# Delta-rule attention and a feed-forward block on one core: loads under a schedule of depths, another model of instruction fetches, and a new order

## The chip, the cores and the metric

The kernel runs on one core of a Trainium2 chip. The metric is the device time of one execution in microseconds (us). Everything below is in us unless marked otherwise.

## The reference

```python
def _attn_ref(q, k, v, beta):            # B, H, S, D = 4, 8, 768, 48
    k_n = k / (np.linalg.norm(k, axis=-1, keepdims=True) + 1e-06)
    state = np.zeros((B, H, D, D), dtype=np.float32)
    for t in range(S):
        kt, vt, bt = (k_n[:, :, t], v[:, :, t], beta[:, :, t, None])
        y[:, :, t] = np.einsum('bhd,bhde->bhe', q[:, :, t], state)
        v_old = np.einsum('bhde,bhd->bhe', state, kt)
        state = state + bt[:, :, :, None] * np.einsum('bhd,bhe->bhde', kt, vt - v_old)
    return y

def _moe_ref(x, w_in, w_out):            # 3072 tokens, 384 -> 2048 -> 384
    h = x @ w_in
    g = h - np.tanh(h)
    return g @ w_out
```

`reference` turns the attention's answer into 3072 rows of 384 numbers and puts them through `_moe_ref`. All inputs and the output are fp32.

## The kernel before

**The work and its pieces.** The 768 steps are cut into 24 chunks of 32 steps, four chunks to a group. A chunk covers 128 tokens (32 steps of 4 batches), a group 512 tokens, which is one window of the feed-forward part. Window 0 is worked in two halves of 256 tokens, the others whole. The 2048 hidden channels are 16 tiles of 128.

**Loads.** All big inputs go through SP's queue (`loads`, L358): keys and queries for the scores (`kc`, `kd`; L315, L322), values (L330), keys in natural order `kt` (L333) and the weights as 32 pieces of 384 KB (`raw`; L354 for `w_in`, L352 for `w_out`). The line `plan.after = plan.flight[-depth[0]][1]` makes a load wait until the load so many places ahead of it has landed; the number is 5 throughout. The planner books each load's time with `transfer` (L263).

**Decoding the weights.** A weight arrives as 8-byte numbers. A piece goes through a Prelu on ScalarE (L814), a byte step on ScalarE (L821) or a shift on VectorE (L824), a word step on VectorE (L826), a cast to the high part (L836, on ScalarE or VectorE) and a subtraction for the low part (L840). Tables by piece (`LOW`, `BYTE`, `CAST`) say which engine.

**The attention.** For each chunk TensorE forms the scores' products k.k and q.k (L406); ScalarE copies them out (L425, L463) or VectorE masks them straight away (L411); the copies are masked by L428. Per group, `solve` (L469) norms the keys (square root on ScalarE, L536), builds a triangular system and solves it on VectorE in pairs of L576 and L578. For group 0 it works in two halves: transposes L589, L594, L598; then for each of its pairs of chunks a join (matmuls L623 and L635, and on VectorE L638, which writes the inverse's off-diagonal block into `tt`). Later groups end in one transpose, L604. The chain then runs chunk by chunk: `keyed` (L681, state times keys), `vsub` (L689), `chunk` (L705), its result copied into `ub` by ScalarE (L721) and VectorE (L723), `update` of the state (L739), copies of the state (L768), the answer (L758) and its copy (L776), and the turn (L792), which is cut into a high part on ScalarE (L799, xh) and a low part on VectorE (L801, xl) for the feed-forward part.

**The feed-forward part.** A hidden block (L869) is nine matmuls of 512 columns (256 in window 0); its gate is tanh on ScalarE (L880), the difference on VectorE (L882), a cast (L888, on either engine) and the rest (L891, VectorE or GpSimd). An out block (L914) is nine more, and the results leave through L945 and L950. Where TensorE has nothing to do, fillers run: L291 (512 columns) and L293 (256), and small pads, L301.

**What sets the order.** The whole program is straight-line code, written out by a planner (`Plan`, L68). Each piece of work is a generator that yields operations with an engine, a cost and what they depend on. The planner emits at each step the operation that can begin first, as adjusted by ranks (`RANKS`, with `TWEAK`, `DUES` and `HOLD` on top). Each engine runs its instructions in the order in which they were emitted. `fetch` (L139) lets a matmul group start later when its instructions reach into a new block of 256, which is taken to arrive after the loads booked so far, but at most 2.2 after the crossing, plus 2.7. `room` and `deep` (L160) say when a load may go out. Tables by tile (`GC`, `GL`, `PREP`) send casts, low parts and the preparing of values to one engine or another.

## Time and profile before

| | us |
|---|---|
| three runs, without a profile | 607.52, 610.75, 609.8 |
| their median | 609.8 |
| the profiled execution | 608.45 |
| its span, first to last instruction | 606.7 |
| around the span | 1.75 |
| TensorE busy in the span | 569.1 (94%) |
| VectorE busy | 364.2 (60%) |
| ScalarE busy | 251.2 (41%) |

The profile comes from one execution, slightly shorter than the median. A row of a timeline gives the start, the length, engine, line, operation, and in brackets the idle time ahead of it with what ended it; "issue" there means nothing that the profile shows. TensorE's and VectorE's busy shares are averages over very different stages: about 61 us of attention alone, some 67 in which the first window's blocks run beside the decoding of the weights, and then the long run of whole windows.

### The profile page before, as it was taken

To read this page: it belongs to the slowest core of one execution; us is meant where nothing else is said; L and a number is where in the kernel's file an instruction comes from. 1 tells how busy PE (TensorE), PEld (TensorE's weight loads), DVE (VectorE), ACT (ScalarE), POOL (GpSimd) and SP (SyncE) were. 2 spreads that over 40 slices of the span, in tenths; PEclk is the share of its full clock that TensorE was granted. 3 is DMA by queue.
4 is the path that set the end of the run, shared out by engine and by line. 5 is a ranking of instruction groups with operands and counts; after the bars stand their busy time and mean duration, and the time that the engine had idled before them with its cause. 6 is when DMAs were issued, how large, how long until landed. Compare 5 with 4: busy or idle time off the path is not lost.

```text
span 606.7 us, 21467 instructions
## 1 busy us (share of the span) xinstructions
PE 569.1 (94%) x9747; PEld 471.5 (78%) x9747; DVE 364.2 (60%) x817; ACT 251.2 (41%) x434; POOL 39.5 (7%) x49
## 2 busy tenths in 40 slices
PE   3567898999999999999999999999999999999997
PEld 3455898989988888777878787787888777887885
DVE  3958799962299932699524998229994232324333
ACT  1546773435443345524354423454324344323332
POOL 1000331001120000010010100001000100000000
PEclk9999899999999999999999999999999999999999
DMA  8986831023321034401234102422001200001001
GB/s 269 300 293 203 283 94 47 14 76 104 111 71 52 1 90 139 124 5 53 75 103 147 32 1 82 134 73 59 1 0 53 73 15 2 1 0 53 1 1 52
DMA packets 25979, 49.88 MB, mean 82 GB/s; under 512 B 3280, under 2 KB 15952, under 8 KB 25888
## 3 DMA queue, kind: packets, MB, share of 16 engines
q1 hardware_dynamic: 25488, 47.95, 25.0%
q8 instruction: 76, 1.25, 0.9%
q10 hardware_dynamic: 400, 0.56, 0.3%
q14 instruction: 15, 0.12, 0.1%
HBM read 43.78 MB, written 4.72 MB: 80 GB/s over the span
## 4 chain that ended last, share of the span: by engine, by line
PE 67%; DVE 21%; DMA 5%; issue 4%; ACT 2%; SPq 0%; ACTq 0%; DVEq 0%
PE ph L869 26%; PE po L914 26%; PE psa L406 4%; DVE ta L576 3%; DVE a L578 3%; PE psu L705 2%; PE psy L758 2%; DVE t L882 2%; PE psk L681 2%; PE sums L739 2%; DVE gh L891 2%; DMA kd<-in_kp 2%; DMA raw<-in_w_in 2%; PE psy L681 2%; DVE a L480 1%
## 5 line engine op out<-in xcount | busy, mean ns | idle before, releaser
L914 PE MATMUL po<-gh,w 128*128 128x512 f32 (+1 forms) x1008 | 218.8, 364 | 1.8 <-ACT o L945 1.0
L869 PE MATMUL ph<-xt,w 128*128 128x512 f32 (+1 forms) x1008 | 216.9, 364 | 2.7 <-DVE t L882 2.0
L869 PEld LDWEIGHTS ph<-xt,w 128*128 128x128 f32 x1008 | 170.0, 190 | 33.6 <-DVE t L882 3.0
L914 PEld LDWEIGHTS po<-gh,w 128*128 128x128 f32 x1008 | 170.0, 190 | 32.4 <-ACT o L945 1.9
L882 DVE TENSOR_TENSOR t<-ph,t 128x512 f32<-128x512 f32 (+1 forms) x112 | 68.5, 612 | 107.0 <-ACT t L880 106.9
L880 ACT ACTIVATE t<-ph 128x512 f32<-128x512 f32 (+1 forms) x112 | 60.2, 537 | 131.6 <-PE ph L869 106.4
L888 ACT CAST gh<-t 128x512 fp32r<-128x512 f32 (+1 forms) x102 | 58.6, 575 | 102.6 <-PE po L914 54.4
L891 DVE TENSOR_TENSOR gh<-t,gh 128x512 fp32r<-128x512 f32 (+1 forms) x107 | 67.6, 633 | 48.8 <-ACT gh L888 48.0
L578 DVE TENSOR_TENSOR a<-a,ta 128x58 f32<-128x58 f32 (+9 forms) x164 | 55.2, 336 | 4.0
L576 DVE TENSOR_TENSOR ta<-a 128x58 f32<-128x58 f32 (+9 forms) x164 | 54.9, 335 | 4.0
L768 ACT COPY st<-sums 48x768 f32<-48x768 f32 x44 | 35.0, 796 | 21.0 <-PE sums L739 19.2
L406 PE MATMUL psa<-kc 48*32 48x64 f32 (+1 forms) x1536 | 28.2, 229 | 11.8 <-issue 8.1
L651 POOL TENSOR_TENSOR v<-v,nt 128x384 f32<-128x384 f32 x21 | 17.8, 854 | 305.3 <-DMA v<-in_vn 299.2
L406 PEld LDWEIGHTS psa<-kc 48*32 48x32 f32 x1536 | 24.2, 119 | 17.2 <-issue 10.4
L721 ACT ACTIVATE ub<-psu,cs 128x384 f32<-128x384 f32 x46 | 24.4, 578 | 24.1 <-PE psu L705 24.1
L705 PE MATMUL psu<-v,tt 32*32 32x48 f32 x1536 | 22.4, 209 | 3.6 <-DVE v L689 3.1
L463 ACT COPY gs<-psa 128x256 f32<-128x256 f32 x20 | 12.3, 614 | 32.6 <-PE psa L406 32.6
L705 PEld LDWEIGHTS psu<-v,tt 32*32 32x32 f32 x1536 | 19.1, 109 | 8.4 <-DVE v L689 4.0
L801 DVE TENSOR_TENSOR xt<-psa,xt 128x384 fp32r<-128x384 f32 x24 | 13.3, 553 | 19.6 <-ACT xt L799 19.6
L739 PE MATMUL sums<-ub,kt 64*48 64x96 f32 x736 | 21.8, 253 | 2.0 <-issue 1.2
L758 PE MATMUL psy<-ub,pc 32*32 32x48 f32 x1536 | 22.6, 208 | 0.4 <-DVE ub L723 0.4
L739 PEld LDWEIGHTS sums<-ub,kt 64*48 64x48 f32 x736 | 16.5, 123 | 8.3 <-issue 6.1
(85 smaller groups left out, 380.8 us busy)
## 6 DMA issues: line engine op xcount, KB each, us to landing
kd<-in_kq SPq DMA_DIRECT2D x23, 448.0 KB, 3.9
kc<-in_kp SPq DMA_DIRECT2D x20, 448.0 KB, 4.8
raw<-in_w_in SPq DMA_DIRECT2D x16, 384.0 KB, 5.3
raw<-in_w_out SPq DMA_DIRECT2D x16, 384.0 KB, 5.8
v<-in_vn SPq DMA_DIRECT2D x24, 192.0 KB, 3.9
kt<-in_kn SPq DMA_DIRECT2D x24, 192.0 KB, 2.7
out<-o SPq DMA_DIRECT2D x17, 256.0 KB, 2.1
kc<-in_kp SPq DMA_DIRECT2D x3, 224.0 KB, 4.9
```

What stands on the lines that cost most here:

```text
L406: nc.tensor.matmul(ps[q, h, :], kc[rows, 0, u, :], kc[rows, x, u, :], start=True, stop=True)
L576: nc.vector.tensor_tensor(tv, P(slice(j + 1, size), slice(j, j + 1)).broadcast_to(dims), top.broadcast_to(dims), ALU.mult)
L578: nc.vector.tensor_tensor(rest_, rest_, tv, ALU.add)
L705: nc.tensor.matmul(pu[rows, h, :], tt[rows, 8 * r + h, :], v[rows, h, :], start=True, stop=True)
L739: nc.tensor.matmul(to, kt[rows, h, :], ub[rows, h], start=(s == 0 and h < 2), stop=True, skip_group_check=True)
L768: (nc.vector.tensor_copy if eng == "DVE" else nc.scalar.copy)(st[rows, :, :, hp, :], ps)
L869: nc.tensor.matmul(p, wi[f][:, a, ct, :], xt[:, b, ct, part], start=(ct == 0 and i == 0), stop=(ct == NC - 1 and i == 2))
L880: nc.scalar.activation(t_, p, AF.Tanh)
L882: nc.vector.tensor_tensor(t_, p, t_, ALU.subtract)
L888: (nc.vector.tensor_copy if on_dve else nc.scalar.copy)(gh[:, 0, :n], t_)
L891: hw_.tensor_tensor(gh[:, 1, :n], t_, gh[:, 0, :n].bitcast(F32), ALU.subtract)
L914: nc.tensor.matmul(po[c][:, part], wo[f][:, a, 128 * c:128 * c + 128], gh[:, b, :n], start=(f == 0 and i == 0 and z < 1), stop=(f == NF - ...
```

## The change

The planner's model of three things changes, and all its tables are replaced.

- `fetch`: a block of instructions now arrives 2.45 after the later of the crossing plus 0.6 and the end of the loads booked so far less 0.4. The bound of 2.2 is gone.
- `room`: the number of loads under way follows the planner's time. It is 5 until 9.9, 2 until 22.25, 3 until 43.47, and 5 after that. In the program as built, the loads from raw 1's first half to raw 1's second half wait for the load two places ahead, those from raw 2's first half to raw 7's second half for three, and the others for five.
- `transfer`: 330 GB/s in place of 290, and 0.85 to land in place of 0.4.
- Constants, ranks, dues and the tables by tile have new numbers. 25 casts of the gate are on VectorE where it was 10, 12 of the rest on GpSimd where it was 5, 5 low parts of weights on GpSimd where it was 4, and 4 values are prepared on VectorE where it was 3. The fillers of 512 columns are 38 where they were 17, those of 256 columns 7 where they were 24, and the pads 16 where they were 34.

All real work is the same. From L160 on a line of the kernel before has a number that is higher by one than in the changed kernel.

```diff
@@ fetch
-            lines.append(max(at + 1.4, min(self.dma[0], at + 2.2)) + 2.7)
+            lines.append(max(at + 0.6, self.dma[0] - 0.4) + 2.45)
@@ room, deep
-        n = self.deep()
-        return self.flight[-n][0] if len(self.flight) >= n else 0.0
-
-    def deep(self):
-        return QUIET if self.calm() else FLIGHT
+        for n, a, b in zip(DEPTHS, (0.0,) + PHASES, PHASES + (1e9,)):
+            t = max(a, self.free["SP"], self.flight[-n][0] if len(self.flight) >= n else 0.0)
+            if t < b:
+                return t, n
@@ transfer
-        plan.dma[0] = max(plan.dma[0], end + 1.5) + kb * 1024e-3 / 290.0
-        return Event(plan.dma[0] + 0.4)
+        plan.dma[0] = max(plan.dma[0], end + 1.5) + kb * 1024e-3 / 330.0
+        return Event(plan.dma[0] + 0.85)
@@ loads
-                    depth[0] = plan.deep()
-                    return plan.room()
+                    t, depth[0] = plan.room()
+                    return t
@@ tables
-FLIGHT, QUIET, FILL0, SOON, HASTE, PADT, RIDE = 5, 5, 1.89, 28.48, 0.4, 13.27, 0.38
+DEPTHS, PHASES = (5, 2, 3, 5), (9.9, 22.25, 43.47)
+FILL0, SOON, HASTE, PADT, RIDE = 1.99, 29.03, 0.13, 19.04, 0.32
-GC = [int(x) for x in "10000110011010000000101000000011"]
+GC = [int(x) for x in "11111011011111110110110110111101"]
-    "score": (-20.93, -84.55, -7.16), "gram": (-38.65, -104.48, -99.64), "solve": (-76.22, -172.04, -61.98),
+    "score": (-46.64, -87.64, -2.97), "gram": (-36.29, -173.12, -95.32), "solve": (-89.51, -149.32, -32.24),
...
```

Three places show how the order moves. The first is the start of solve(0). On ScalarE, from its seventh instruction on, before (`psa` is a product in PSUM, `pc` its copy, `nm` the norm, `raw0` weight piece 0):

```order
L536 ACTIVATE nm_289<-ss_290 128x32
L425 COPY pc_336<-psa_252 128x256
L814 ACTIVATE raw0_247<-raw0_247 128x768
L547 ACT_TABLE_LOAD
L547 ACTIVATE wz_79<-wz_79 128x1
L821 ACTIVATE raw0_247<-raw0_247,cs_76 128x768
```

And now:

```order
L424 COPY pc_328<-psa_250 128x256
L535 ACTIVATE nm_286<-ss_287 128x32
L424 COPY pc_368<-psa_295 128x256
L813 ACTIVATE raw0_247<-raw0_247 128x768
L820 ACTIVATE raw0_247<-raw0_247,cs_76 128x768
```

Two copies of products are ahead of piece 0's Prelu where it was one, and one of them is ahead of the square root. On VectorE, from the building of the triangle (L561) on, before (`a0` is the triangle, `ta` its scratch):

```order
L561 SCALAR_TENSOR_TENSOR a0_287<-a0_287,gm_293 128x16x16 x2
L576 TENSOR_TENSOR ta_78<-a0_287 128x28
L578 TENSOR_TENSOR a0_287<-a0_287,ta_78 128x2x14
L576 TENSOR_TENSOR ta_78<-a0_287 128x52
L578 TENSOR_TENSOR a0_287<-a0_287,ta_78 128x2x13x2
L576 TENSOR_TENSOR ta_78<-a0_287 128x72
```

And now, with piece 0's word, cast and low part (`w0`) in between:

```order
L560 SCALAR_TENSOR_TENSOR a0_284<-a0_284,gm_290 128x16x16 x2
L825 SCALAR_TENSOR_TENSOR raw0_247<-raw0_247 128x768
L575 TENSOR_TENSOR ta_78<-a0_284 128x28
L577 TENSOR_TENSOR a0_284<-a0_284,ta_78 128x2x14
L835 CAST w0_406<-raw0_247 128x2x384
L575 TENSOR_TENSOR ta_78<-a0_284 128x52
L577 TENSOR_TENSOR a0_284<-a0_284,ta_78 128x2x13x2
L839 TENSOR_TENSOR w0_406<-raw0_247,w0_406 128x2x384
L575 TENSOR_TENSOR ta_78<-a0_284 128x72
```

Two masks (L410) and piece 1's word follow further down in the same solve, all ahead of its first transpose. The second place is VectorE behind the solve, from the first transpose to the first join of `tt`, before (`v` are values, `pc` scores, `raw` and `w` weights):

```order
L589 STREAM_TRANSPOSE tt0_506<-a0_287 128x16x32
L594 STREAM_TRANSPOSE ta_78<-a0_287 128x16x32
L598 STREAM_TRANSPOSE tt0_506<-a0_287 128x16x32
L651 TENSOR_TENSOR v_100<-v_100,nt_294 128x384
L651 TENSOR_TENSOR v_137<-v_137,nt_294 128x384
L428 TENSOR_TENSOR pc_432<-pc_432,cs_76 128x256
L428 TENSOR_TENSOR pc_460<-pc_460,cs_76 128x256
L824 TENSOR_SCALAR raw3_438<-raw3_438 128x768
L826 SCALAR_TENSOR_TENSOR raw0_247<-raw0_247 128x768
L428 TENSOR_TENSOR pc_336<-pc_336,cs_76 128x256
L638 SCALAR_TENSOR_TENSOR tt0_506<-psa_593,cs_76,tt0_506 128x8x16
```

And now:

```order
L588 STREAM_TRANSPOSE tt0_579<-a0_284 128x16x32
L593 STREAM_TRANSPOSE ta_78<-a0_284 128x16x32
L597 STREAM_TRANSPOSE tt0_579<-a0_284 128x16x32
L650 TENSOR_TENSOR v_99<-v_99,nt_291 128x384
L427 TENSOR_TENSOR pc_404<-pc_404,cs_76 128x256
L427 TENSOR_TENSOR pc_368<-pc_368,cs_76 128x256
L427 TENSOR_TENSOR pc_328<-pc_328,cs_76 128x256
L650 TENSOR_TENSOR v_103<-v_103,nt_291 128x384
L839 TENSOR_TENSOR w1_585<-raw1_292,w1_585 128x2x384
L823 TENSOR_SCALAR raw3_581<-raw3_581 128x768
L825 SCALAR_TENSOR_TENSOR raw2_478<-raw2_478 128x768
L637 SCALAR_TENSOR_TENSOR tt0_579<-psa_671,cs_76,tt0_579 128x8x16
```

A third mask, a low part and a word of piece 2 stand ahead of the first join where piece 0's word stood, and piece 3's shift is still among them. The third place is TensorE around the first chunks, before from update 0 on (`psa` from `tt0` and `yj` are the joins, `psk` and `psy` with `st` the keyed products):

```order
L739 MATMUL sums_80<-ub_677,kt_102 48x2x48 x16
L623 MATMUL psa_705<-tt0_506,gs0_89 32x16 x32
L758 MATMUL psy_744<-ub_677,pc_432 32x48 x32
L792 MATMUL psa_783<-cs_76,y_sb_779 128x128 x3
L635 MATMUL psa_790<-yj_777,ta_78 32x16 x32
L291 LDWEIGHTS wz_79
L291 MATMUL po0_82<-wz_79 128x512
L681 MATMUL psk_842<-st_77,kd1_175 32x96 x16
L681 MATMUL psy_843<-st_77,kd1_175 32x96 x16
L705 MATMUL psu_891<-v_137,tt0_506 32x48 x32
```

And now, from the first join's matmuls to chunk 0:

```order
L622 MATMUL psa_592<-tt0_579,gs0_89 32x16 x32
L622 MATMUL psa_629<-tt0_579,gs0_89 32x16 x32
L634 MATMUL psa_671<-yj_667,ta_78 32x16 x32
L634 MATMUL psa_713<-yj_709,ta_78 32x16 x32
L290 LDWEIGHTS wz_79
L290 MATMUL po0_82<-wz_79 128x512
L704 MATMUL psu_748<-v_99,tt0_579 32x48 x32
```

Both joins now stand ahead of chunk 0; the second one's matmuls stood between update 0 and keyed 1.

## Rows read from the trace of the kernel before

**Rows 1.** Table of stretches: start and end, length, then the busy time of TensorE, its weight loads, VectorE, ScalarE and GpSimd (with instructions), the granted TensorE clock, the DMA engines' busy share, and GB/s.

```profile
0.00:61.28 61.28, 37.22 (x1337) 28.15 (x1337) 41.07 (x89) 27.82 (x41) 3.18 (x10) 1.00 0.82 264
64.07:127.69 63.62, 60.16 (x1193) 56.76 (x1194) 58.79 (x150) 32.01 (x63) 11.55 (x9) 0.97 0.30 98
127.69:600.00 472.31, 466.35 (x7189) 382.49 (x7189) 260.71 (x576) 187.61 (x324) 22.80 (x29) 1.00 0.18 56
```

**Rows 2.** TensorE's waits from 0 to 110: what waited, for what, total us, times, longest.

```profile
PE psa L406 <- issue: 10.3, 4, 3.9
```

**Rows 3.** The page's DMA queues: packets, MB, share of 16 engines.

```profile
q8 instruction: 76, 1.25, 0.9%
```

**Rows 4.** TensorE's timeline, the scores' products and the first join: start, length, line, idle ahead in brackets.

```profile
19.42 1.60 PE L406 MATMUL psa<-kc 48*32 48x32 f32 x99 [3.87 <-issue]
...
32.36 0.58 PE L406 MATMUL psa<-kc 48*32 48x64 f32 x10 [3.69 <-issue]
32.87 1.10 PE L623 MATMUL psa<-tt,gs 32*32 32x16 f32 x64
```

**Rows 5.** VectorE's timeline, solve(0) and its first join.

```profile
16.71 0.20 DVE L576 TENSOR_TENSOR ta<-a 128x28 f32<-128x28 f32 x1
...
25.28 1.06 DVE L589 STREAM_TRANSPOSE tt<-a 128x512 f32<-128x512 f32 x1
...
36.84 0.35 DVE L638 SCALAR_TENSOR_TENSOR tt<-psa,cs,tt 128x128 f32<-128x128 f32 x1 [5.51 <-PE psa L635]
```

**Rows 6.** TensorE's timeline from chunk 0 to the first hidden block.

```profile
37.25 1.50 PE L705 MATMUL psu<-v,tt 32*32 32x48 f32 x64 [0.48 <-DVE tt L638]
...
40.11 1.53 PE L739 MATMUL sums<-ub,kt 64*48 64x96 f32 x32 [0.81 <-DVE ub L723]
...
49.47 1.51 PE L681 MATMUL psk<-st,kd 112*32 112x96 f32 x32
...
59.45 1.10 PE L406 MATMUL psa<-kc 48*32 48x64 f32 x64
...
61.28 2.42 PE L869 MATMUL ph<-xt,w 128*128 128x256 f32 x18
```

**Rows 7.** VectorE's instructions from 28 to 62, grouped by line: busy us, mean ns of one, idle ahead.

```profile
L826 DVE SCALAR_TENSOR_TENSOR raw<-raw 128x768 int32<-128x768 int32 x9 | 8.6, 956 | 0.0
L840 DVE TENSOR_TENSOR w<-raw,w 128x768 fp32r<-128x768 f32 x7 | 6.7, 954 | 0.1
L824 DVE TENSOR_SCALAR raw<-raw 128x768 int32<-128x768 int32 x4 | 2.3, 564 | 0.0
L836 DVE CAST w<-raw 128x768 fp32r<-128x768 f32 x4 | 2.2, 552 | 0.0
...
L428 DVE TENSOR_TENSOR pc<-pc,cs 128x256 f32<-128x256 f32 x3 | 1.2, 435 | 0.0
L801 DVE TENSOR_TENSOR xt<-psa,xt 128x384 fp32r<-128x384 f32 x2 | 1.1, 558 | 1.1 <-ACT xt L799 1.1
...
L651 DVE TENSOR_TENSOR v<-v,nt 128x384 f32<-128x384 f32 x2 | 1.0, 544 | 0.0
```

**Rows 8.** ScalarE's timeline around solve(0), and the state's copy after update 0.

```profile
13.79 0.23 ACT L536 ACTIVATE nm<-ss 128x32 f32<-128x32 f32 x1 [10.02 <-DVE ss L511]
15.19 0.37 ACT L425 COPY pc<-psa 128x256 f32<-128x256 f32 x1 [1.17 <-PE psa L406]
15.77 0.89 ACT L814 ACTIVATE raw<-raw 128x768 f32<-128x768 f32 x1 [0.21 <-DMA raw<-in_w_in]
...
18.09 0.96 ACT L821 ACTIVATE raw<-raw,cs 128x768 int32<-128x768 uint8 x1
...
43.20 0.79 ACT L768 COPY st<-sums 48x768 f32<-48x768 f32 x1 [1.33 <-DVE st L768]
```

**Rows 9.** All 16 loads of `w_in`, time from issue to landing.

```profile
DMA to landing us min/median/max: 3.5/5.3/7.1
```

**Rows 10.** VectorE's instructions from 64 to 128, grouped by line: busy us, mean ns of one, idle ahead.

```profile
L882 DVE TENSOR_TENSOR t<-ph,t 128x256 f32<-128x256 f32 x21 | 8.7, 417 | 0.5 <-ACT t L880 0.5
...
L888 DVE CAST gh<-t 128x256 fp32r<-128x256 f32 x6 | 1.7, 289 | 0.0
```

**Rows 11.** TensorE's timeline near the end of window 0's overlap, and chunk 4.

```profile
122.85 1.24 PE L914 MATMUL po<-gh,w 128*128 128x256 f32 x9
123.93 2.32 PE L869 MATMUL ph<-xt,w 128*128 128x256 f32 x18
...
131.02 0.88 PE L705 MATMUL psu<-v,tt 32*32 32x48 f32 x64
```

**Rows 12.** TensorE's timeline at the end of window 0: the last turn and what follows it.

```profile
172.60 0.55 PE L792 MATMUL psa<-cs,y_sb 128*128 128x128 f32 x3
172.91 4.79 PE L869 MATMUL ph<-xt,w 128*128 128x256 f32 x27
```

**Rows 13.** TensorE's weight loads, timeline, at the last out block.

```profile
600.82 1.68 PEld L914 LDWEIGHTS po<-gh,w 128*128 128x128 f32 x8 [0.33 <-DVE gh L891]
```

**Rows 14.** SP's timeline, three issues: start, length in the queue, what is loaded.

```profile
27.56 5.74 SPq L315 DMA_DIRECT2D kc<-in_kp  x2
...
54.56 0.33 SPq L330 DMA_DIRECT2D v<-in_vn  x1
61.41 0.33 SPq L333 DMA_DIRECT2D kt<-in_kn  x1
```

More of the change, by code (lines that the diff above doesn't have):

```diff
@@ L1009 @@
+GL = [int(x) for x in "11010101101000000000101000110010"]
 BYTE = [int(x) for x in "1110111001010111"]
-PREP = [int(x) for x in "0010"]
-CAST = [int(x) for x in "1011001010010000"]
-GC = [int(x) for x in "10000110011010000000101000000011"]
+PREP = [int(x) for x in "0000"]
+CAST = [int(x) for x in "1010011010100000"]
+GC = [int(x) for x in "11111011011111110110110110111101"]
 RANKS = {
-    "mask": (-32.37, -37.91, 7.1), "answers": (-14.24, -55.53, -1.28), "moved": (29.15, -23.48, -15.77),
-    "score": (-20.93, -84.55, -7.16), "gram": (-38.65, -104.48, -99.64), "solve": (-76.22, -172.04, -61.98),
-    "join": (-0.8, 19.48, 32.82), "prep": (-62.42, 24.49, 50.59), "keyed": (-78.17, -12.19, -47.04),
-    "chunk": (-3.89, 32.79, 20.73), "update": (21.42, -29.13, -22.09), "answer": (55.51, 34.26, 60.41),
-    "vsub": (-41.91, -5.88, 54.2), "spread": (-38.17, -40, 8.2), "keep": (8.64, 39.88, 21.97),
-    "y": (23.84, 0.77, 57.29), "turn": (-10.04, -17.53, 8.95), "xh": (-11.76, 23.09, 117.67),
-    "xl": (12.12, -26.31, 22.22), "raw": (-49.09, -24.09, -28.31), "word": (-7.84, -79.58, -20.8),
-    "high": (9.94, -11.13, -38.28), "low": (11.13, -23.86, 42.85), "hidden": (21.81, -34.31, -15.76),
-    "out": (-34.25, -11.58, -0.19), "tanh": (-21.22, 10.97, 42.16), "lw": (-32.26, -8.41, -32.05),
[3 rows of a table removed]
@@ L1026 @@
-HOLD = [11.87, 1.73, 0]
+    "mask": (-51.4, -25.44, -4.49), "answers": (-11.29, -23.17, -37.84), "moved": (82.62, -19.37, -94.63),
+    "score": (-46.64, -87.64, -2.97), "gram": (-36.29, -173.12, -95.32), "solve": (-89.51, -149.32, -32.24),
+    "join": (14.87, -22.33, 84.36), "prep": (-50.27, -23.5, 58.14), "keyed": (-110.02, -19.62, -21.59),
+    "chunk": (-39.43, 13.76, 9.17), "update": (9.24, -7.15, -20.24), "answer": (15.23, 56.56, 16.95),
+    "vsub": (25.27, -6.27, 39.52), "spread": (-32, -48.21, -32.63), "keep": (-35.35, -16.32, 63.96),
@@ L1027 @@
+    "y": (16.21, 29.92, 104.72), "turn": (-12.05, -15.64, 30.52), "xh": (-50.88, 7.05, 53.86),
+    "xl": (5.76, -71.85, 42.14), "raw": (-39.7, 4.39, -0.22), "word": (7.02, -7.26, 33.55),
+    "high": (7.19, -7.02, -1.45), "low": (26.91, -44.7, 47.28), "hidden": (37.9, -28.65, -41.88),
+    "out": (-12.65, -18.77, -7.35), "tanh": (-54.48, -15.76, 34.42), "lw": (-18.65, -49.35, -9.34),
[3 rows of a table added]
+HOLD = [9.94, 36.8, 0]
 DUES = {
-    "x0": 9.364, "x1": 31.018, "x2": 63.17, "x3": 85.053, "x4": 121.817, "r4": 5.942, "p4": 87.319, "u0": 56.841,
@@ L1036 @@
-    ("chunk", 2): -11.69, ("chunk", 3): -39.11, ("chunk", 4): 19.01, ("chunk", 5): 6.92, ("chunk", 6): -6.29,
+    ("answers", 9): -0.02, ("answers", 10): 0.14, ("answers", 11): 4.34, ("chunk", 0): -46.83, ("chunk", 1): 22.61,
+    ("chunk", 2): -26.82, ("chunk", 3): -32.39, ("chunk", 4): 19.01, ("chunk", 5): 6.92, ("chunk", 6): -6.29,
     ("chunk", 7): 1.2, ("chunk", 8): -1.87, ("chunk", 9): 4.69, ("chunk", 10): -5.27, ("chunk", 11): -0.1,
-    ("gate", -1): 5.11, ("gate", 0): 30.18, ("gate", 1): -9.36, ("gh", -1): -2.8, ("gh", 0): -22.27,
@@ new lines @@
+    ("moved", 11): -0.74, ("out", -1): 3.94, ("out", 0): -17.63, ("out", 1): 4.98, ("prep", 0): 16.17,
+    ("prep", 1): -44.38, ("prep", 2): 2.09, ("prep", 3): -77.75, ("prep", 4): -0.23, ("prep", 5): -5.22,
+    ("prep", 6): -0.07, ("prep", 7): 3.65, ("prep", 8): -3.06, ("prep", 9): 0.51, ("prep", 10): -2.75,
+    ("prep", 11): -0.01, ("raw", 0): -9.18, ("raw", 1): -3.4, ("raw", 2): -27.43, ("raw", 3): -6.13,
+    ("raw", 4): -45.36, ("raw", 5): -7.67, ("raw", 6): 43.75, ("raw", 7): -8.14, ("raw", 8): 20.28,
@@ new lines @@
+    ("raw", 9): -28.37, ("raw", 10): -28.85, ("raw", 11): -13.28, ("raw", 12): -82.62, ("raw", 13): 6.46,
+    ("raw", 14): -25.43, ("raw", 15): 10.45, ("score", 0): 0.11, ("score", 1): 2.47, ("score", 2): -1.45,
+    ("score", 3): 1.9, ("score", 4): 17.38, ("score", 5): 19.28, ("score", 6): -10.65, ("score", 7): 47.27,
+    ("score", 8): -0.02, ("score", 9): -5.02, ("score", 10): 1.82, ("score", 11): -2.03, ("solve", 0): -6.69,
+    ("solve", 4): 50.53, ("solve", 8): -55.42, ("solve", 12): -76.11, ("solve", 16): -28.82, ("solve", 20): -48.75,
```

134 lines of the change are left out of this document (62 added, 72 removed), and 74 rows, old and new, of tables (RANKS, TWEAK).

## The prediction

> **What bounds the kernel now.** I read the table of stretches first [rows 1]. From 127.69 to 600.00 TensorE is busy 466.35 of 472.31 us: nothing but its own work counts there, and the change neither adds to nor takes from that work. The loss lies ahead. Up to the first hidden block at 61.28 TensorE is busy 37.22 us, fillers included, and from 64.07 to 127.69 VectorE is busy 58.79 of 63.62 us. So the sum is about two things: when the first hidden block starts, and how long VectorE's queue is between there and chunk 4.
>
> Next I read what TensorE waited for early on [rows 2]. The largest entry, 10.3 us, is "issue" ahead of the products: the engine waited for nothing that has a semaphore. In TensorE's own sequence [rows 4] such a wait stands inside a group of equal matmuls (99 of the scores' products after 3.87 us at 19.42, 10 more after 3.69 us at 32.36), where the next instruction, not its data, is missing. I take these as waits for the next block of instructions: a queue of its own brings them, 76 packets of together 1.25 MB or 16 KB each [rows 3], and meanwhile the loads keep the DMA engines busy (share 0.82 up to 61.28 [rows 1]). The change's depths and its new fetch line bear on this.
>
> Third comes the chain to the first hidden block: solve(0) on VectorE from 16.71, its first transpose ending at 25.28 + 1.06 = 26.34 [rows 5], joins from 32.87 [rows 4], chunk 0 at 37.25, update 0 at 40.11, keyed 1 at 49.47, hidden at 61.28 [rows 6].
>
> **Step 1, up to the first transpose of solve(0).** Before, that transpose ends at 26.34 and the joins still wait until 32.87 for the block; only the block counts. The change moves weight decoding into VectorE's part of the solve: two words at 0.956, one cast at 0.552, one low part at 0.954 [rows 7], and two masked products, taken like L428 at 0.435: 1.91 + 0.55 + 0.95 + 0.87 = +4.3. On ScalarE the copy of one score (15.19, 0.37) now precedes the square root, which stood at 13.79 [rows 8]: the root goes to 15.56, +1.8. And the first word needs raw 0's Prelu (0.89) and byte (0.96) [rows 8], which now stand behind a second copy, of a product behind the block that came at 19.42. That block's wait shows no price for its new place. Between all but 0.5 of its 3.87 us removed and none, it comes at 16.0 to 19.4; I take 17.5, the middle, since five loads are still in flight there. With 0.7 for its product (44 of the 99 matmuls that took 1.60), 0.37, 0.89 and 0.96 the word starts at 20.4, where VectorE would otherwise be ready at 16.71 + 1.8 = 18.5: 1.9 idle (0.4 to 3.8). The transpose ends at 26.34 + 4.3 + 1.8 + 1.9 = **34.3** (32.8 to 36.2). Two loads in flight then should bring the block of 32.36 well before that; TensorE's extra 512-column fillers lie in that wait. It would count again only if it came after 34.3. So the block wait is replaced by VectorE, and the joins start 1.4 later than 32.87. GpSimd gains low parts of later windows, hidden.
>
> **Step 2, to chunk 0.** Before the first join of tt on VectorE (L638, 36.84) there now stand two more transposes (1.06 each), two values (0.544 each), three masks (0.435), a low part, a shift (0.564) and a word: 2.1 + 1.1 + 1.3 + 0.95 + 0.56 + 0.96 = 7.0 [rows 5, 7], and the join's 0.35: chunk 0 at 34.3 + 7.3 = **41.6** (40 to 43.5), 4.4 after before's 37.25. Both joins' matmuls run beneath it. Depth 2 holds SP, and behind it stand raw 1's second half, the keys of chunks 6 and 7 and raw 2, whose word is due at about 40. Raw 0 lands by 15.77 [rows 8]; nine loads of 393 or 459 KB at 264 GB/s [rows 1] take some 15, and raw 2 is there by 32. If two in flight starve the engines (5.3 from issue to landing [rows 9], so 2.65 a load), it comes at 40 and chunk 0 slips by up to 2; that is the upper bound.
>
> **Step 3, chunk 0 to the first hidden block.** Before: 61.28 - 37.25 = 24.0. There keyed 1 at 49.47 stood behind joins, answer and turn, while the state was ready at 43.20 + 0.79 = 43.99 [rows 6, 8]: 5.5. After, both joins are already done and three fillers (some 0.6) stand there: -4.9. The product at 59.45 (1.0 from its start to the next) moves behind the hidden block: -1.0. So 18.1, and hidden starts at 41.6 + 18.1 = **59.7**, -1.6 (55.5 to 62.5).
>
> **Step 4, hidden block to chunk 4.** VectorE has more ahead of solve(1)'s end than before: six more L882 at 0.417 and fourteen more casts L888 at 0.289 [rows 10], two words, a low part, two shifts and a cast [rows 7], less one L891: 2.5 + 4.05 + 1.9 + 0.95 + 1.1 + 0.55 - 0.5 = 10.6. By this queue chunk 4 comes at 131.02 - 1.6 + 10.6 = 140.0. But TensorE has also done 12 more hidden and out half blocks by then; one takes 123.93 - 122.85 = 1.08 [rows 11], 13.0 in all. At equal progress chunk 4 would come at 144.0, so VectorE's sum says -4.0. If TensorE kept all of its idle time there, only step 3's -1.6 would stay. VectorE is busy 92% of this stretch, so I take -3.5, near its end (-6 to +1, with step 3's bounds).
>
> **Steps 5 and 6.** At the end of window 0, three half blocks of window 0 (172.91, x27) stand between the last turn (172.60) and the next window [rows 12]; in the changed order none do. The hidden block then waits for two casts, about 0.56 each by L801 [rows 7], and their hand-overs: +1.3. At the end, the last out block waits for its gate until 600.82, with five fillers ahead [rows 13]; in the changed order three other out blocks stand before it: -0.95. 330 GB/s and 0.85 of landing are planner's numbers and cost nothing by themselves; the gates moved from ScalarE to VectorE after 131 lie under TensorE.
>
> **The sum.** -3.5 + 1.3 - 0.95 = -3.15 on the profiled execution's 608.45 (606.7 of span and 1.75 around it): 605.3. The median of the three runs is 1.35 higher, so 606.65.
>
> **Rivals.**
> A, faster: short fetches and small groups at their later pace. The 64 small matmuls of a chunk took 1.50 at 37.25 and 0.88 at 131.02 [rows 6, 11], although the clock column reads 1.00 in the row that covers the first and in that of the second [rows 1]; I can't say from these rows why. If fillers (17 of 512 columns become 38) bring the small groups to the later pace, eight groups between chunk 0 and hidden (chunks, updates, keyed, answers) give 8 x 0.6 = 4.9, and no idle in step 1 gives 1.5 more. Hidden at 53 to 54; with about 5 of it kept, 601.5. Against it: the fillers stand ahead of the joins and thin out behind them.
>
> B, slower: the loads end too late. SP issues in order, and the changed order has 13 weight loads behind kt of chunk 3 where it was 8; that kt waits for update 1, just ahead of the hidden block (61.41, where the load before it went at 54.56 [rows 14]). Five loads of 393 KB at 264 GB/s [rows 1] are 7.4 us. ScalarE has the Prelus of these weights in order between its tanhs, so the gates stall with them. It decides from the point where a weight lands after ScalarE reaches its Prelu; then 606.65 + 7.4 = 614. For it: at depth 3 an issue-to-landing time of 3.5 to 7.1 [rows 9] gives one load per 1.2 to 2.4, and SP has stood for 5.74 on two loads already (27.56). Against it: late weights may find other blocks to run.
>
> C, no change: the schedule doesn't shorten the fetches. The block arrives at 19.42 as before, the first transpose ends at 36.2, hidden is at 61.6 and step 4 leaves -1.6 instead of -3.5: 608.5. Or the block does come early, and TensorE keeps its idle time in step 4: -1.6 too, and 608.5.
> Two rules of the Trainium skill speak for C. Its page "Runtime: NRT & Kernel Launch", section "Instruction fetch mechanics", calls the price of crossing a block boundary "mostly hidden"; the 10.3 us of [rows 2] disagree. Its page "DMA: Bandwidth & Descriptors", section "Queues, rings and completion order", has each DMA engine take turns between its queues packet by packet, so that a fetch would not stand behind all loads in flight; by that, 608.5.
>
> **How the numbers follow.** Forecast 0.42 (604.5 to 608.2), A 0.18, C 0.16, B 0.22, something slower elsewhere 0.02. A measurement of this kernel tells about 0.5% from no change, here 606.75 and 612.85. Faster: A and 0.27 of the forecast, 0.45. Same: 0.15 of the forecast and C, 0.31. Slower: 0.24. The range of 601 to 613.5 leaves out half of A and half of B. Forecast: 606.6.
>
> **What would show it.** Step 1: the "issue" waits ahead of products fall from 10.3 to under 6, and VectorE's first transpose of solve(0) ends near 34.3. Step 2: chunk 0 at 41.6. Step 3: hidden at 59.7. Step 4: chunk 4 near 140.5. Step 5: TensorE idle about 1.3 at the first hand-over. Small groups at 0.88 early show A; ScalarE idle on DMA between tanhs shows B; an issue wait of over 3.5 us near 19 or 32 shows C. The forecast is wrong if VectorE is not what ends solve(0), or if chunk 4 is after 143.

## The result, and the profile after

| | before | after |
|---|---|---|
| median, us | 609.19 | 616.49 |
| runs | 4, 607.52 to 610.75 | 4, 614.70 to 618.30 |
| the profiled execution, us | 608.45 | 616.44 |
| its span, us | 606.7 | 614.7 |

The ratio is 1.012 (95% interval 1.0079 to 1.0161): the change makes the kernel slower by 7.3 us. The prediction said 606.6, with a range of 601.0 to 613.5, and gave slower 0.24. It was wrong: the kernel got slower, by more than the range allowed. In the changed kernel, lines from L160 on have a number one lower than before.

The table of stretches over the same boundaries as [rows 1], with the same columns (busy times of TensorE, its weight loads, VectorE, ScalarE and GpSimd, granted clock, DMA share, GB/s):

```profile
0.00:61.28 61.28, 36.68 (x1305) 25.85 (x1306) 35.27 (x81) 24.07 (x38) 2.35 (x9) 0.81 0.76 231
...
64.07:127.69 63.62, 59.33 (x1193) 56.51 (x1192) 57.54 (x141) 34.96 (x61) 18.19 (x14) 0.97 0.43 136
127.69:600.00 472.31, 459.61 (x7151) 378.25 (x7150) 268.26 (x595) 183.83 (x314) 26.44 (x33) 1.00 0.18 56
```

The last row is the surprise. After 127.69 TensorE was taken to be full in both kernels; it is busy 459.61 us where it was 466.35. So most of the loss comes after the stages that the sum was about.

TensorE's waits from 0 to 110, the three largest entries "issue" (to be set against [rows 2]):

```profile
PE psa L405 <- issue: 4.2, 2, 2.2
PE psy L757 <- issue: 4.0, 1, 4.0
PE psa L634 <- issue: 2.7, 1, 2.7
```

Ahead of the products such waits fell from 10.3 to 4.2 us, but 4.0 and 2.7 us of them now stand in the chain, at an answer and at a join. TensorE's timeline up to the first hidden block (against [rows 4, 6]) shows where:

```profile
17.37 1.59 PE L405 MATMUL psa<-kc 48*32 48x32 f32 x99 [2.25 <-issue]
...
32.30 1.93 PE L405 MATMUL psa<-kc 48*32 48x64 f32 x64 [3.25 <-DMA kc<-in_kp]
...
40.55 1.26 PE L634 MATMUL psa<-yj,ta 16*32 16x16 f32 x78 [2.69 <-issue]
...
42.28 1.24 PE L704 MATMUL psu<-v,tt 32*32 32x48 f32 x49
...
57.88 1.40 PE L757 MATMUL psy<-ub,pc 32*32 32x48 f32 x57 [4.00 <-issue]
...
63.12 1.10 PE L868 MATMUL ph<-xt,w 128*128 128x256 f32 x7
```

VectorE's timeline (against [rows 5]): the word and a masked product in solve(0), its first transpose, the first join's write to `tt`, and the transpose that ends solve(1):

```profile
20.21 0.96 DVE L825 SCALAR_TENSOR_TENSOR raw<-raw 128x768 int32<-128x768 int32 x1 [2.29 <-ACT raw L820]
...
27.90 0.42 DVE L410 TENSOR_TENSOR pc<-psa,cs 128x256 f32<-128x256 f32 x1 [0.64 <-ACT gs L462]
...
32.62 1.10 DVE L588 STREAM_TRANSPOSE tt<-a 128x512 f32<-128x512 f32 x1
...
41.02 0.35 DVE L637 SCALAR_TENSOR_TENSOR tt<-psa,cs,tt 128x128 f32<-128x128 f32 x1 [1.40 <-PE psa L634]
...
139.99 2.09 DVE L603 STREAM_TRANSPOSE tt<-a 128x1024 f32<-128x1024 f32 x1
```

And TensorE's timeline from chunk 4 to the last turn of window 0 and the first block of window 1 (against [rows 11, 12]):

```profile
145.66 0.88 PE L704 MATMUL psu<-v,tt 32*32 32x48 f32 x64
...
149.98 0.79 PE L757 MATMUL psy<-ub,pc 32*32 32x48 f32 x53 [1.07 <-issue]
...
154.06 1.09 PE L405 MATMUL psa<-kc 48*32 48x64 f32 x63 [0.40 <-issue]
...
159.16 1.11 PE L913 MATMUL po<-gh,w 128*128 128x256 f32 x8 [2.88 <-issue]
...
160.53 1.41 PE L738 MATMUL sums<-ub,kt 64*48 64x96 f32 x32
161.87 1.50 PE L757 MATMUL psy<-ub,pc 32*32 32x48 f32 x64
163.30 1.71 PE L868 MATMUL ph<-xt,w 128*128 128x256 f32 x9
164.93 0.87 PE L680 MATMUL psk<-st,kd 112*32 112x96 f32 x32
...
172.75 0.88 PE L738 MATMUL sums<-ub,kt 64*48 64x96 f32 x32
...
175.64 0.87 PE L680 MATMUL psk<-st,kd 112*32 112x96 f32 x32
...
180.42 1.00 PE L913 MATMUL po<-gh,w 128*128 128x256 f32 x7 [0.98 <-issue]
...
184.85 0.55 PE L791 MATMUL psa<-cs,y_sb 128*128 128x128 f32 x3 [0.22 <-ACT y_sb L775]
185.97 4.29 PE L868 MATMUL ph<-xt,w 128*128 128x512 f32 x16 [0.57 <-ACT xt L798]
```

Four issue waits, 1.07 + 0.40 + 2.88 + 0.98 = 5.33 us, where the trace of before has 0.92 between 128 and 190. The third stands inside a group of nine equal matmuls: one had run, eight were not there yet. Behind it the table of stretches shows a lower granted clock (0.66 in the second row, so the level of 1.2 GHz for a part of it), after TensorE was busy for 2.12 of 5 us:

```profile
155.00:160.00 5.00, 2.12 (x83) 1.89 (x73) 0.42 (x1) 1.65 (x3) 0.00 (x0) 1.00 0.67 214
160.00:165.00 5.00, 5.00 (x115) 4.33 (x117) 0.56 (x1) 2.54 (x4) 0.83 (x1) 0.66 0.15 46
```

**Where the 8.0 us of span come from.** In TensorE's order window 0 has 64 half blocks (hidden and out, 256 columns). Before, 41 stand ahead of chunk 4, 18 between chunk 4 and the last turn, 5 behind it. After: 53, 10 and 1. Chunk 4 starts 145.66 - 131.02 = 14.64 later [rows 11]. The stretch from there to the last turn takes 184.85 - 145.66 = 39.19, before 172.60 - 131.02 = 41.58 [rows 12]: 2.39 less. Behind the turn stand four half blocks fewer, at 1.08 [rows 11] 4.32 less. 14.64 - 2.39 - 4.32 = +7.93, nearly the whole difference of the spans. The eight half blocks that left the stretch are 8.64 us of work, and it became only 2.39 us shorter: 6.25 us were lost there. Ahead of chunk 4 stand 12 half blocks more, 12.96 us of work, and it comes 14.64 later: 1.68 more were lost there.

The trace tells what fills the 6.25 us. Issue waits are 4.41 more than before (5.33 against 0.92). The update, the answer and the hidden block behind the longest wait took 4.40 us, from 160.53 to 164.93; the same three groups one chunk later, at the full clock, took 2.89, from 172.75 to 175.64. So the lower clock cost 1.51. Waits for VectorE (0.18, at 170.83) and ScalarE (0.22) add 0.40. Together that is 6.3.

### The profile page after: what moved, and what is told of

It is laid out like the page before. It is cut to its first block, busy times and chain, and to the rows that moved or that the text cites. A ratio compares the mean times of both kernels' runs of the same rounds, so it can differ in the third digit from the quotient of the medians.

```text
span 614.7 us, 21438 instructions
## 1 busy us (share of the span) xinstructions
PE 569.3 (93%) x9733; PEld 471.2 (77%) x9733; DVE 367.7 (60%) x825; ACT 247.1 (40%) x419; POOL 48.6 (8%) x56
## 4 chain that ended last, share of the span: by engine, by line
PE 79%; DVE 10%; issue 5%; ACT 3%; DMA 3%; SPq 0%; ACTq 0%; DVEq 0%
PE ph L868 30%; PE po L913 29%; PE psa L405 4%; PE psy L757 3%; PE psu L704 3%; PE sums L738 3%; PE psk L680 2%; PE psy L680 2%; DMA kd<-in_kp 2%; PE po L290 1%; PE psa L791 1%; DVE t L881 1%; DVE gh L890 1%; DMA kc<-in_kp 1%; DVE a L577 1%
## 5 line engine op out<-in xcount | busy, mean ns | idle before, releaser
L890 DVE TENSOR_TENSOR gh<-t,gh 128x512 fp32r<-128x512 f32 (+1 forms) x100 | 63.4, 634 | 63.1 <-ACT gh L887 63.0
L887 ACT CAST gh<-t 128x512 fp32r<-128x512 f32 (+1 forms) x87 | 52.6, 605 | 99.8 <-PE po L913 81.0
L757 PE MATMUL psy<-ub,pc 32*32 32x48 f32 x1536 | 24.0, 212 | 6.5 <-issue 5.4
L757 PEld LDWEIGHTS psy<-ub,pc 32*32 32x32 f32 x1536 | 20.1, 112 | 10.7 <-issue 6.6
```

The lines of the kernel that those rows point to most:

```text
L757: nc.tensor.matmul(py[rows, h, :], pc[rows, h, :], ub[rows, h, b % 2, :], start=(s == 0), stop=True, skip_group_check=True)
L887: (nc.vector.tensor_copy if on_dve else nc.scalar.copy)(gh[:, 0, :n], t_)
L890: hw_.tensor_tensor(gh[:, 1, :n], t_, gh[:, 0, :n].bitcast(F32), ALU.subtract)
```

## The experiments

The theory: the loss comes from the stretch from chunk 4 to window 1. Small groups use up instructions faster than blocks of them arrive, and the half blocks between them are the cover; the new order takes 8 of 18 away. Rivals: the depths (loads in front of the fetches), VectorE's longer queue early on, and the prediction's own view that TensorE is full there. Unless the text says otherwise, a kernel is the program of before or after with every instruction kept in its place on its engine, and the edit shown. The diffs tell most edits in short words (`HID` a hidden and `OUT` an out half block); in the kernels they are lists of the program's order. Ratios are to the kernel before, run beside it; line numbers can differ by a few.

**How fast blocks of instructions come (m_fetch).** Small products alone, a weight load and a matmul each, without and with loads under way:

```diff
+for depth, wide in ((0, 0), (2, 0), (3, 0), (5, 0), (0, 9), (5, 9)):   # loads under way, wide matmuls per group
+    loads of 448 KB, each waiting for the one `depth` places ahead
+    24 groups of products, L406's shapes, each followed by `wide` matmuls of 512 columns
```

> TensorE alone, the attention and the feed-forward part are left out: stages of 24 groups of 128 instructions (32 small fp32 products of 64 columns, two passes each): no loads; 448 KB loads 2, 3 and 5 deep; then again without loads and 5 deep with nine wide matmuls (1.94 us) behind each group. Theory A: without loads a block of 256 instructions takes 3.4 to 3.7 us although its matmuls need 2.1; with loads 2 deep 3.7 to 4.3, 5 deep 4.4 to 5.2; with the wide matmuls no waits without loads. Rival (only the loads make TensorE wait): without loads 2.1 us a block.

One execution, 391.48 us. TensorE's timeline: first without loads, then two under way, then five, then five with the wide matmuls between:

```profile
13.31 1.99 PE L73 MATMUL ps<-kc 48*32 48x64 f32 x128 [1.47 <-issue]
16.77 1.99 PE L73 MATMUL ps<-kc 48*32 48x64 f32 x128 [1.47 <-issue]
...
88.08 3.64 PE L73 MATMUL ps<-kc 48*32 48x64 f32 x128 [0.89 <-issue]
92.36 3.63 PE L73 MATMUL ps<-kc 48*32 48x64 f32 x128 [0.64 <-issue]
...
172.93 3.63 PE L73 MATMUL ps<-kc 48*32 48x64 f32 x128 [2.16 <-issue]
179.40 3.64 PE L73 MATMUL ps<-kc 48*32 48x64 f32 x128 [2.84 <-issue]
...
332.95 1.44 PE L73 MATMUL ps<-kc 48*32 48x64 f32 x56 [2.55 <-issue]
```

Each row of 128 matmuls goes with 128 weight loads, 256 instructions: a block. Its matmuls take 1.99 us, and without loads the next block is there 3.45 to 4.00 us after the last one (3.46 in the rows shown). With two loads under way it is 4.0 to 4.8 (4.28 here), with five 5.9 to 6.5 (6.47 here), more than the 4.4 to 5.2 that were expected. (The rows of 3.63 ran at the lower clock, so the spacing is what to compare.) With the wide matmuls between and no load there were no such waits: that is what cover is. With five loads under way the same cover was not enough, and three waits of 0.57 to 2.55 us are left. One chunk of attention is some 580 instructions or 2.3 blocks. By the spacing without loads that is about 8 us (an estimate), where its own matmuls take 5.2 at the full clock, summed from start to start in the trace of before.

**The depths (after_depth5, before_depths, after_late3, before_late3).**

```diff
 after_depth5, after's order:
-depths 5 x8, 2 x5, 3 x16, then 5
+depths 5
 before_depths, before's order:
-depths 5
+depths 5 x8, 2 x5, 3 x16, then 5
 after_late3, after's order from raw 8, before_late3, before's order from raw 6, both to the values of chunk 6:
-depth 5
+depth 3
```

> The changed kernel in its own order, instruction by instruction, with all loads 5 deep. Theory A (TensorE waits for instruction blocks wherever small groups stand too densely; the depth of the loads matters little): the time stays within 2 us of the changed kernel, 614.5 to 618.5; the early block waits grow by 1 to 3 us, and the keys of chunk 6 (a DMA wait of 3.25 us at 32.30) come earlier. Theory B (the schedule of depths costs the time): back to 609 to 612.

> The kernel before in its own order, with the depths of the changed kernel by the load's place in the queue (8 loads 5 deep, 5 loads 2 deep, 16 loads 3 deep, the rest 5 deep). Theory A: within 2 us of the kernel before, 607 to 611. Theory B: 4 to 8 us slower, 613 to 617.

> The changed kernel in its own order, but the loads that went 5 deep after the schedule's last step (from weight 16 on, up to the values of chunk 6) go 3 deep. Theory A with the depths of the block experiment (5.0 us a block at 3 deep, 6.1 at 5 deep): the wait of 4.00 us ahead of the answer at 57.88 falls to 2 to 3 us, the first hidden block comes 1 to 2 us earlier; the weights come later, so the whole is 0 to 2 us faster. Rival (that wait has nothing to do with the loads): it stays at 4 us and the whole is the same or slower.

> The kernel before in its own order; the loads from weight piece 12 on up to the values of chunk 6 go 3 deep where they went 5 deep. Theory A: the block waits at 42.97 and 48.07 (0.98 and 1.09 us) shrink to 0.6 or less in sum, the first hidden block comes up to 1.5 us earlier, and the whole is 0.5 to 2 us faster, 606.5 to 608.2. Rival (the weights come later and the gates wait for them): the same or up to 3 us slower.

after_depth5: 618.12, ratio 1.0155 (1.0111 to 1.02). before_depths: 611.15, 1.0045 (1.002 to 1.007). after_late3: 613.34, 1.0066 (1.0032 to 1.0101). before_late3: 609.32, 0.9997 (0.9977 to 1.0018). Without the schedule the new order is not faster, so the schedule doesn't make the loss, as theory A had it; the early issue waits, though, stayed as they were (11.6 us up to 62, in the changed kernel 11.4). On before's order the schedule costs 0.45%: issue waits up to 62 fall from 13.1 us (9.8 of them ahead of the products) to 8.2, and TensorE's waits for the loads of `kc` rise from 3.0 to 6.8. Depth 3 for later loads changes nothing on before's order, against what was expected. On after's order the kernel was faster, but its interval overlaps that of the changed kernel. The answer of chunk 1 waited 0.44 there where it was 4.00, and hidden began at 59.22. That doesn't show the depth as the cause: with depth 5 kept, that answer waited 0.98 in after_spread and 2.4 in after_wide, and with depth 3 it waited 1.5 in after_late3_spread.

**Cover put back (after_spread, after_late3_spread).** An out block and a hidden block, with their gates, go back from ahead of keyed 4 into chunks 4 and 5: 12 half blocks in the stretch.

```diff
-OUT f8, HID f11 ahead of keyed 4
+OUT f8 behind keyed 4, HID f11 behind chunk 4; gates of f10 and f11 with them
```

> The changed kernel in its own order but for two half blocks of window 0 (one out, one hidden, with its gate) that move from ahead of keyed 4 to between the groups of chunk 4 and chunk 5. Theory A: the block waits at 149.98, 154.06 and 159.16 (1.07, 0.40 and 2.88 us) fall to under 2 us in sum, and the whole is 2 to 4 us faster than the changed kernel. If density is not the cause: within 0.7 us of the changed kernel.

> The changed kernel with both repairs: the late loads 3 deep (3.2 us faster alone) and the two half blocks spread among chunks 4 and 5 (3.8 us faster alone). If they are two separate causes they add: 609 to 611. If both repaired the same wait: 612 to 613.5.

after_spread: 612.68, 1.0082 (1.0056 to 1.0109); issue waits from 128 to 190 fall from 5.33 to 2.95 us. after_late3_spread: 613.19, 1.0065 (1.0044 to 1.0086). The direction is the theory's, but the interval of after_spread overlaps that of the changed kernel, so the time alone doesn't prove it, and with depth 3 the two gains don't add up. The stretch itself says more. TensorE's timeline of after_spread, chunk 4 and the last turn:

```profile
142.61 0.88 PE L703 MATMUL psu<-v,tt 32*32 32x48 f32 x64
...
180.41 0.55 PE L790 MATMUL psa<-cs,y_sb 128*128 128x128 f32 x3 [0.21 <-ACT y_sb L774]
```

It takes 37.80 us with two half blocks (2.16 us) more in it, and 37.50 in after_late3_spread. With the order of the changed kernel it takes 39.19, and 42.87, 37.99 and 37.74 in after_depth5, after_late3 and after_front, which leave the order of that stretch as it is. So 2.16 us of work went in and the stretch became no longer.

**Instructions taken away (after_wide, before_wide, before_wide_pad).** The products of chunks 8 to 11 stand in this stretch. Eight matmuls of 256 columns take the place of 32 of 64, which leaves other numbers in those scores; before_wide_pad puts 64 tiny matmuls behind chunk 11's products.

```diff
-for u in range(16): two matmuls of 64 columns      # a half of a chunk's heads
+for pr in range(2): for h in (0, 4): two matmuls of 256 columns   # chunks 8 to 11
+64 x matmul of 32 columns behind chunk 11          # before_wide_pad alone
```

> The changed kernel in its own order; only the score products of chunks 8 to 11 (four groups between the chunks of group 1) are issued as 8 matmuls of 256 columns in place of 32 of 64: the same columns, engine time and dependencies, a quarter of the instructions (and scores that are not the reference's, for those chunks). Theory A (the stretch from chunk 4 to chunk 7 is bound by the arrival of instruction blocks): TensorE's issue waits between 145 and 186, 5.3 us in sum, fall below 1.5, and the whole is 3 to 6 us faster than the changed kernel's 616.5: 610.5 to 613.5. Rival (the chain of a chunk, keyed to update, is what takes 9 to 10 us): under 1 us faster.

> The same edit in the kernel before, in its own order. There only one issue wait (0.92 us) lies between chunk 4 and chunk 7. Theory A: 0 to 1.5 us faster than the kernel before. If fewer instructions help by themselves: as much as in the changed kernel.

> The kernel before with wide scores, which lost 4.2 us although it has less to do, and had 5.1 us of issue waits after 186 where the kernel before has 0.3. Added: 64 pads of 32 columns (about 2.1 us, they add zeros) behind chunk 11's scores. The wide scores took out 384 instructions, one block and a half; with 128 for the pads it is one whole block, so that all later instructions stand at their old places in the blocks. Theory P (what was lost is the place of the block boundaries: the order had them under wide work, the shift puts them into small groups): the issue waits after 186 fall below 1.5 us and the whole is 2 to 4 us faster than with wide scores alone, 608.5 to 611. If the place doesn't matter: the pads cost their 2 us, 614 to 615.5.

after_wide: 612.67, 1.006 (1.004 to 1.008); issue waits from 128 to 190 are 1.61 us, just above the 1.5 expected, and the time is in theory A's range. Chunk 4 and the last turn in its timeline of TensorE:

```profile
146.25 0.88 PE L712 MATMUL psu<-v,tt 32*32 32x48 f32 x64
...
180.62 0.55 PE L799 MATMUL psa<-cs,y_sb 128*128 128x128 f32 x3 [0.21 <-ACT y_sb L783]
```

The stretch takes 34.37 us, 4.82 less than in the changed kernel, at a granted clock of 1.00, with the same half blocks in it; a group of products takes 1.08 us as it did with narrow matmuls (1.10). So 4.82 of the 6.25 us lost there come back when instructions are taken away and the work stays. The rival, that the chain of a chunk takes the time by itself, is refuted for that part.

before_wide: 612.85, 1.0064 (1.0042 to 1.0085), against what was expected. Its trace has waits from 190 to 600 where before has 0.29 us:

```profile
PE psy L766 <- issue: 3.2, 5, 1.0
PE psu L713 <- issue: 1.9, 4, 0.7
```

384 instructions fewer are one and a half blocks, so each later block boundary fell half a block away from its old place in the program. before_wide_pad adds 128 instructions, the shift becomes one whole block, and the waits go: 608.45, 0.9995 (0.9976 to 1.0015). More instructions, less time: the place of the boundaries counts, not only their number.

**VectorE's queue (after_front).** The decoding of pieces 0 and 1 goes behind the joins, the products of chunk 6 behind the first join.

```diff
-solve(0): word, cast, low part of raw 0 and word of raw 1 between the pairs; low part of raw 1 and words of raw 2, 3 before the join
+all of them behind the join of chunk 1
```

> The changed kernel, with the decoding of weight pieces 0 and 1 moved on VectorE from inside solve(0) to behind the first two joins, and the products of chunk 6 on TensorE behind the first matmuls of the joins. If VectorE is what sets chunk 0 (the prediction's steps 1 and 2): the first transpose ends at 28 to 29 instead of 33.7, chunk 0 is at 35 to 36.5 instead of 42.3, and the whole is 4 to 6 us faster. Theory A (instruction blocks set it): the transpose moves as much, but chunk 0 comes at 37.5 to 40, the first hidden block 1 to 3 us earlier, and the whole is 1 to 3 us faster.

621.66, 1.0217 (1.0178 to 1.0256): slower, where both theories had it faster. VectorE's timeline:

```profile
31.10 0.42 DVE L409 TENSOR_TENSOR pc<-psa,cs 128x256 f32<-128x256 f32 x1 [6.73 <-ACT gs L461]
...
35.08 1.04 DVE L587 STREAM_TRANSPOSE tt<-a 128x512 f32<-128x512 f32 x1
```

With the decoding gone the first transpose comes no earlier: VectorE waits 6.73 us for a product, which on TensorE stands behind 18 fillers. Eleven of these took 4.15 us here and 2.55 in the changed kernel, so part of that wait is the lower clock. In the changed kernel VectorE waits for the same product too, 0.64 at 27.90: the decoding had filled a wait.

**The stretch of before made dense (before_bunch).** Seven half blocks move from chunks 6 and 7 to behind the last turn, so that 11 are left.

```diff
 TensorE, before's order, chunk 6 and 7
-... update answer HID10 HID11 HID12 OUT10 keyed products chunk OUT11 OUT12 turn update answer HID13 turn HID14 ...
+... update answer keyed products chunk turn update answer turn HID10 HID11 HID12 OUT10 OUT11 OUT12 HID13 HID14 ...
```

> The order of the kernel before, with one stretch made as dense as the changed kernel's: the hidden blocks and out blocks of pieces 10, 11 and 12 and the hidden block of piece 13, seven half blocks of window 0, move with their gates from chunks 6 and 7 to behind the turn of chunk 7. From chunk 4 to that turn 11 half blocks are left, where before has 18 and the changed kernel 10. No work is added or left out. Theory (cover against instruction blocks): the issue waits between 128 and 190 rise from 0.96 to 3 to 5 us, the turn of chunk 7 comes less than 7 x 1.08 = 7.6 us earlier, and the kernel is 2.5 to 5 us slower than before, 611 to 614. Rival (TensorE is full there and the place of a block costs nothing, as step 4 and the sum of the prediction had it): the turn of chunk 7 comes 7.6 us earlier and the time is that of before, 608 to 610.

614.30 us, 1.0116 (1.0085 to 1.0147): one edit in the order of before costs as much as the whole change. TensorE's timeline, and the table of stretches behind it:

```profile
130.15 0.88 PE L704 MATMUL psu<-v,tt 32*32 32x48 f32 x64
...
163.07 0.71 PE L704 MATMUL psu<-v,tt 32*32 32x48 f32 x48 [1.32 <-issue]
...
167.79 0.44 PE L757 MATMUL psy<-ub,pc 32*32 32x48 f32 x20 [1.33 <-issue]
168.80 0.55 PE L791 MATMUL psa<-cs,y_sb 128*128 128x128 f32 x3 [0.57 <-ACT y_sb L775]
169.11 4.97 PE L868 MATMUL ph<-xt,w 128*128 128x256 f32 x27
```
```profile
160.00:165.00 5.00, 3.03 (x156) 2.33 (x149) 3.26 (x5) 1.74 (x4) 1.26 (x1) 1.00 0.61 184
165.00:170.00 5.00, 3.10 (x104) 2.69 (x105) 2.66 (x13) 2.33 (x4) 0.00 (x0) 0.94 0.33 90
170.00:175.00 5.00, 5.00 (x34) 5.00 (x33) 1.74 (x5) 1.85 (x5) 0.12 (x1) 0.72 0.00 0
```

Chunk 4 starts 0.87 earlier than before in this execution, and the last turn comes at 168.80, 3.8 earlier [rows 11, 12]. So the stretch is 2.93 us shorter for 7.56 us of work taken out of it: 4.63 are lost. TensorE idles 3.9 of the 10 us from 160 to 170, and the granted clock falls behind that. The issue waits (3.52 us from 128 to 190, 2.6 more than before) are as expected. The time is 7.0 above before where 2.5 to 5 were, because two things had no price in the expectation. The chain's own waits for ScalarE and VectorE are 2.2 us from chunk 4 to the turn. Behind the turn 3.0 more are lost, about 1.5 of them at the lower clock: the three hidden half blocks there took 4.97 us, three others in before (at 158.79, at the full clock) 3.49. The rival, TensorE full there, is refuted.

**Parts of the change, planned anew (before_fetchline, after_oldline).** Here the planner writes its own order.

```diff
 before_fetchline, in before:
-            lines.append(max(at + 1.4, min(self.dma[0], at + 2.2)) + 2.7)
+            lines.append(max(at + 0.6, self.dma[0] - 0.4) + 2.45)
 after_oldline, in after: the reverse
```

> One part of the change alone, the planner's new fetch line (and with it the order that it gives) in the kernel before, with its tables, depths and transfer line. 18 half blocks of window 0 stand between chunk 4 and the turn of chunk 7, as before. Theory (the stretch's cover decides): no issue waits to speak of there, and the time is that of before within 3 us, 607 to 612. Rival (the new fetch line makes the slow order): 614 or more.

> The changed kernel with the old fetch line: tables, depths and transfer line are the new ones. 11 half blocks stand between chunk 4 and the turn of chunk 7, and 45 instead of 53 ahead of chunk 4. Theory (the stretch's cover decides): issue waits of 3 us and more between 128 and 190, and 613 to 619. Rival (the new fetch line makes the slow order): 607 to 611, with issue waits there of under 1.5.

before_fetchline: 623.08, 1.0238 (1.0192 to 1.0284). after_oldline: 618.55, 1.0176 (1.014 to 1.0212). Both missed the theory. The rival's figure came for before_fetchline and not for after_oldline. before_fetchline keeps 18 half blocks in the stretch and is slower still; TensorE's timeline, and a row of the table of stretches:

```profile
68.47 2.42 PE L869 MATMUL ph<-xt,w 128*128 128x256 f32 x18
...
161.37 1.51 PE L739 MATMUL sums<-ub,kt 64*48 64x96 f32 x26 [1.42 <-issue]
...
164.24 5.15 PE L869 MATMUL ph<-xt,w 128*128 128x256 f32 x27
```
```profile
160.00:170.00 10.00, 8.63 (x124) 8.27 (x125) 1.92 (x5) 3.81 (x8) 0.00 (x0) 0.66 0.17 49
```

Its hidden block comes 7.2 later than before's, and nine of the 18 half blocks stand together between chunks 6 and 7 (the 27 matmuls are the first three), so the chunks ahead of them are dense again. From chunk 4 to the last turn it takes 46.41 us with the same 18 half blocks for which before needs 41.58. after_oldline is in its range for another reason than the one given: its issue waits from 128 to 190 are 1.12 us, and from 62 to 128 they are 4.64; its chunk 4 comes 10.65 later than before's for 4.32 us of work done ahead. So the number of half blocks doesn't tell the time of an order; how they lie between the small groups, at each place, does. Neither the line alone nor the tables alone give an order as good as before's.

## Why the prediction was wrong

**Step 1** held in size: the block came at 17.37 (17.5 forecast), the word waited 2.29 (1.9), the first transpose ended at 32.62 + 1.10 = 33.72 (34.3). Its reason held only in part: VectorE was busy most of the time, but it waited 0.64 at 27.90 for a product behind TensorE's 18 fillers, and after_front, without the decoding in the solve, has the transpose no earlier. The step had put these fillers at nothing ("TensorE's extra 512-column fillers lie in that wait"). The joins began at 35.13, behind two fillers and a product that waited 3.25 for its keys.

**Step 2** held in size (42.28, forecast 41.6), and that was luck: VectorE's queue, which the step added up, was done at 39.62, and the first join's L637 then waited 1.40 for TensorE. There a block wait of 2.69 stood inside the joins' second matmuls, which no term had.

**Step 3** failed: 63.12 instead of 59.7. Chunk 0 to hidden took 20.84, not 18.1. The issue waits did fall ahead of the products, as step 1 asked, but up to 62 only from 13.1 to 11.4 in all: what is no longer waited for at one place is waited for further down, in the chain. The term lacked the 4.00 at the answer of chunk 1. m_fetch shows that loads under way space the blocks further apart; that they made this wait is not shown, since it varies from 0.44 to 4.00 among executions of this order. Two of them have hidden at 61.31 and 64.30.

**Step 4** is the step that decided. VectorE's queue ended later than counted, with hidden (142.08 for solve(1), chunk 4 at 145.66, forecast 140.5): 5.2, of which 3.4 came with hidden. The larger error is in the method: "equal progress" took 12 half blocks done ahead as 13.0 us gained. Four of them came off the end and paid 4.3; eight came out of the stretch behind and paid 2.4 of 8.6. With that priced, the forecast's own -3.5 would have been +2.8, and with the 5.2 by which chunk 4 came later still, +7.9. The first part of the prediction, "TensorE is busy 466.35 of 472.31 us: nothing but its own work counts there", made the error: a busy share of 99% tells that the order of before had cover for each wait, not that another order has. Both of the prediction's own signs of being wrong came: VectorE alone didn't end solve(0), and chunk 4 was after 143.

**Step 5** was 0.57 where 1.3 was taken. It also misread its row: the 27 matmuls at 172.91 are two half blocks of window 0 (18 matmuls of 256 columns) and the first block of window 1 (9 of 512), not three half blocks. **Step 6**: the last out block doesn't wait in the trace of after; its worth was not measured alone.

**The rivals.** A didn't come: the granted clock was 0.81 up to 61.28 and many small groups still took 1.2 to 1.5; three, from 49.50 to 51.13, took 0.84 to 0.88. That clock isn't the change's doing, for executions of before's order show anything from 0.75 (before_late3) to 1.00 there. B didn't either: from 62 to 128 ScalarE waited for weights 2.0 us, not 7.4. C's block did come early. The slower side came by a mechanism that stood in none of them ("something slower elsewhere" had 0.02), although its parts were in the rows: 64 small matmuls and their weight loads in 0.88 us, and a block of 256 that is waited for.

Rival C's two rules fare like this. The Trainium skill, page "Runtime: NRT & Kernel Launch", section "Instruction fetch mechanics", has the price of a boundary mostly hidden: that holds in the kernel before after 128 (1.2 us of issue waits from there to 600) and not where small groups are dense (1.47 us a block in m_fetch without any load). The Trainium skill, page "DMA: Bandwidth & Descriptors", section "Queues, rings and completion order", has each DMA engine take turns between its queues. m_fetch agrees in part: five loads of 448 KB at the 284 GB/s of that stage are 8 us (an estimate), and a block came at most 3.0 later than without loads, so it didn't stand behind all of them. But it came later with five loads in the one queue of SP than with two (6.47 and 4.28), which turns between queues alone don't tell.

**What stays open.** From chunk 4 to the last turn the account closes: most of the 6.25 us are missing instructions and the lower clock behind them, and after_wide, with fewer instructions, won 4.82 back (its edit also moves the later block boundaries, and from 190 on it had 3.8 us of issue waits where the changed kernel had 2.7). Open is how much the chain's own waits on ScalarE and VectorE would take if no block were waited for: they stand in the same gaps, and were 0.40 us in the changed kernel and 2.2 in before_bunch. Open is also what made chunk 4 come 1.68 us later than the work ahead of it asks. And no version was found that beats the kernel before.
